# Moving small transfers to the end of a recurrence step, and splitting an attention product in two

## The chip, the cores and the metric

One core of one Trainium2 chip runs the whole kernel. The metric is the device time of one execution in microseconds (us). A ratio is the mean time of one kernel's fast runs divided by that of the kernel before in the same rounds on the same chip, so it is not quite the ratio of the medians quoted beside it. Intervals are 95%. Sets of experiments fell on different chips; therefore ratios, not times, are compared across sets.

## The reference

Half of the program is a recurrence over 64 segments of 32 tokens. Each segment's attention input has 8 memory rows ahead of its own 32, and the output's first 8 rows are the next segment's memory. The other half is an FFN, which the change does not touch.

```python
def _A_ref(x, mem0, Wq, Wk, Wv, Wo, seg_len):      # B=1, S=2048, Dm=1024, H=32, Dh=128, M=8, seg_len=32
    mem = mem0
    for s in range(n_seg):                         # 64 steps, each needs the mem of the one before
        h = jnp.concatenate([mem, x[:, s*32:(s+1)*32]], axis=1)
        q, k, v = (jnp.einsum('btd,dhe->bhte', h, W) for W in (Wq, Wk, Wv))
        scores = jnp.where(mask, jnp.einsum('bhqe,bhke->bhqk', q, k) * scale, -1e9)
        o = jnp.einsum('bhqk,bhke->bhqe', _softmax(scores), v)
        o = jnp.einsum('bhte,hed->btd', o, Wo)
        mem = o[:, :8].copy(); outs.append(o[:, 8:])
# ... b = gelu(x @ w_gate) * (x @ w_up) @ w_down;   out = g*a + (1-g)*b with g = sigmoid((x*gate_w).sum(-1))
```

## The kernel before

A step has two halves of 16 heads. Each weight matrix half is eight pieces of 512 KB. Not all 64 pieces fit in SBUF: 12 slots are shared by the two halves, and each of them is refilled once a step, when its first use in the step is over. These 12 pieces (6.3 MB) are the stream.

```python
PAIRS = {"k": (0, 2), "q": (0, 2), "v": (0, 1, 2, 4, 6), "o": (0, 2, 4)}      # pieces whose two halves share a slot
ORDER = (("k", 0), ("q", 0), ("v", 0), ("k", 1), ("q", 1), ("o", 0), ("v", 1), ("o", 1))
# half 0 takes the shared pieces first, half 1 takes them last; odd steps swap the halves
def spent(k):
    n = home[k]; done[n] += 1
    if done[n] < len(uses[n]) and uses[n][done[n]] != k:
        fetch(n)                                  # SP issues the next piece for this slot
```

Rows whose k, q and v do not depend on the recurrence (the last 8 of a segment, "rest" rows) are projected four segments at a time by extra PE work, the fills, spread over the steps. Their results go to DRAM scratch (qk_scr, v_scr) and come back when their segment is due (qkr, vB). So a step also has small transfers, all issued by POOL: hT, qkr (two), vB, a_scr, o_scr, the fill stores, and in some steps oR and hR.

The names: hT is the step's input, transposed; hR the rest rows of four segments; qkr and vB the rest rows' q and k, and v. tok is the copy of a projection's result that PE transposes into kT and qT; vA is that of v. E8 are the exponentials, pA and pB the softmax weights (pB for the rest columns), tA and tB their transposes. oT is attend's result, oRc its rest rows, which go to o_scr and come back as oR; a_scr takes the step's output rows, a_bf.

```python
def scores(r):                                    # ... PE: scores, DVE: max, subtract, ACT: exp into E8, DVE: sum, reciprocal
    pB <- E8 * sm (rest columns); pA <- E8 * sm; tA <- transpose(pA); tB <- transpose(pB)      # all DVE, in this order

def attend(u):
    def f(e):
        for j in range(4):
            for g in range(4):                    # main part: 16 matmuls with 32 rows
                e.matmul(PB[bo[g]][...], lhsT=vA[r, j, :], rhs=tA[...], start=(j == 0), stop=False)
        for g in range(4):                        # tail: the rest rows
            ins = e.matmul(PB[bo[g]][...], lhsT=vB[r, u, :], rhs=tB[...], start=False, stop=True)
        return ins
    op("pe", f, rd=[vA.r(), tA.r(), tB.r(), vB.r()], wr=[BK(b) for b in bo])
    # ... four copies to oT (ACT, DVE), one to oRc (POOL)

# a step's schedule: on(matrix, half, piece, work ahead of that piece)
on("k", 0, 5, lambda: load_v(s))
on("v", 0, 4, lambda: trans(qT))
on("k", 1, 3, lambda: rest_k(1))                  # POOL copies the rest keys from qkr into kT
on("q", 1, 0, lambda: load_h(s + 1))
on("q", 1, 1, lambda: load_qk(s + 1, 0))
on("v", 1, 2, lambda: load_qk(s + 1, 1))
on("q", 1, 4, lambda: trans(kT))
on("o", 0, 0, some(f1, 4)); on("o", 0, 0, lambda: attend(ua)); on("o", 0, 0, some(f1, 1))
on("o", 1, 0, lambda: rest_k(0))
on("o", 1, 0, some(f2, 5)); on("o", 1, 0, lambda: attend(ub)); on("o", 1, 0, some(f2))
```

"attend(0)" and "attend(1)" below are the first and the second attend of a step. A group of fill work is four matmuls.

## Time and profile before

| | before |
|---|---|
| median time | 2303.5 us (2301.8 to 2305.6, 4 runs) |
| time a step in the recurrence (steps 8 to 59) | 24.45 us |
| PE idle, 165 to 1660 us | 127.5 of 1495 us |
| bytes streamed a step | 6.3 MB in 12 pieces |

The window sums of the kernel before over most of the recurrence. Each column is an engine's busy time and, in brackets, its instructions; then the granted clock, the DMA share and the bandwidth.

```profile
core 0: us, PE busy (x) PEld busy (x) DVE busy (x) ACT busy (x) POOL busy (x), PEclk, DMA share, GB/s
165.00:1660.00 1495.00, 1367.52 (x31932) 778.54 (x31924) 568.19 (x1629) 430.30 (x982) 543.95 (x1011) 0.99 0.80 287
```

PE is busy 91% of the time, so a step is first of all a row of PE work, with about 2.1 us of gaps. What ends the gaps ahead of matmuls that read weight pieces is in the tile view of `sl` (us in total, times):

```profile
its engine sat idle before it (us, times) until:
  issue: 56.0, 61
  DMA sl<-in_A_Wq_dram: 18.4, 28
  DMA sl<-in_A_Wo_dram: 7.2, 13
  DMA sl<-in_A_Wv_dram: 6.8, 11
  ACT oT L576: 1.7, 4
  DMA sl<-in_A_Wk_dram: 1.3, 2
```

Pieces that come late cost 33.7 us. "Issue" is a gap in which no wait shows. Counted from the packed trace, 53 of the 61 lie between two matmuls of one piece, where the program has no wait at all, and all 61 end 1.2 to 1.6 us after the end of a 16 KB packet on the instruction queue (251 such packets in this window).

One step cut into five windows:

```profile
1142.00:1144.00 2.00, 1.52 (x26) 0.70 (x30) 0.34 (x2) 0.45 (x2) 0.74 (x2) 1.00 0.00 0
1144.00:1148.00 4.00, 4.00 (x76) 1.74 (x64) 0.42 (x1) 1.19 (x2) 2.93 (x6) 1.00 0.78 199
1148.00:1158.00 10.00, 10.00 (x282) 6.26 (x282) 5.17 (x14) 2.73 (x6) 2.39 (x5) 1.00 1.03 406
1158.00:1162.00 4.00, 3.99 (x99) 2.22 (x92) 2.88 (x9) 1.03 (x2) 2.75 (x5) 1.00 0.99 348
1162.00:1166.40 4.40, 3.84 (x113) 2.45 (x114) 0.90 (x4) 1.54 (x5) 2.29 (x5) 1.00 0.46 161
```

DMA is full (1.03, 0.99) in the middle of the step and idle (0.00) around its end. That idle stretch is what the change aims at. The DMA issues of the small loads show what they meet in the middle (KB each, median us from issue to landing):

```profile
qkr<-qk_scr POOLq DMA_DIRECT2D x128, 64.0 KB, 5.4
hT<-xq_scr POOLq DMA_DIRECT2D x64, 64.0 KB, 5.7
vB<-v_scr POOLq DMA_DIRECT2D x63, 64.0 KB, 6.0
```

And attend(1) on PE in the timeline (start us, us, then the instructions):

```profile
1160.76 1.25 PE L697 MATMUL pb<-sl,hR 128*32 128x512 bf16 x20
1161.94 0.27 PE L641 MATMUL pb<-tA,vA 32*128 32x40 bf16 x16
1162.06 0.19 PE L646 MATMUL pb<-tB,vB 32*128 32x64 bf16 x4
1162.18 0.83 PE L697 MATMUL pb<-sl,hR 128*32 128x512 bf16 x12
1162.84 2.18 PE L682 MATMUL pb<-sl,oT 128*32 128x256 bf16 x64
```

### The profile page before, as it was taken

What the parts mean: (1) busy time and instruction counts of PE and PEld (TensorE: products, weight loads), DVE (VectorE), ACT (ScalarE), POOL (GpSimd) and SP (SyncE); (2) the same over time, 40 slices, a digit from 0 to 9 for tenths busy, and PEclk for the clock granted to TensorE, in tenths of its full rate; (3) what the DMA queues carried; (4) which work ended last, traced back from release to release, by engine and by line L of the source; (5) the groups of instructions that cost most, each with busy time, mean ns of one, the idle gap of its engine ahead of it and who ended that gap; (6) DMA issues with size and microseconds to landing.
All of it is one profiled execution on the core that took longest, in us unless ns stands there. A gap on an engine that the chain in (4) does not pass through costs nothing.

```text
span 2304.5 us, 80168 instructions
## 1 busy us (share of the span) xinstructions
PE 2060.9 (89%) x36594; PEld 1099.2 (48%) x36614; DVE 901.2 (39%) x2164; ACT 604.1 (26%) x1280; POOL 616.0 (27%) x1107
## 2 busy tenths in 40 slices
PE   2588998899999998898998998998879999999998
PEld 1244555555555555555555455554444444444443
DVE  3134333334334343343343433333335164363452
ACT  1122232222323222232232322222223032131230
POOL 5233333343333433333333333333210000000000
PEclk9999999999999999999999999999999999999999
DMA  9968788788788787787887887887782802606206
GB/s 358 379 213 305 257 304 294 261 289 309 265 303 302 272 316 271 269 322 265 290 323 248 302 302 256 302 303 266 270 330 90 276 34 80 230 1 208 103 1 237
DMA packets 225714, 576.45 MB, mean 250 GB/s; under 512 B 30424, under 2 KB 42584, under 8 KB 225376
## 3 DMA queue, kind: packets, MB, share of 16 engines
q1 hardware_dynamic: 189536, 513.35, 61.7%
q0 software_dynamic: 26624, 44.14, 5.6%
q10 hardware_dynamic: 9216, 13.83, 1.7%
q8 instruction: 287, 4.70, 0.8%
q14 instruction: 51, 0.42, 0.1%
HBM read 539.71 MB, written 31.39 MB: 248 GB/s over the span
## 4 chain that ended last, share of the span: by engine, by line
PE 65%; DMA 24%; issue 5%; DVE 3%; ACT 2%; POOL 1%; SPq 0%; ACTq 0%; POOLq 0%; DVEq 0%
PE pb L670 20%; PE pb L929 14%; DMA sl<-in_A_Wq_dram 11%; PE pb L682 9%; PE pb L697 6%; PE pb L966 6%; DMA sl<-in_A_Wo_dram 5%; PE pb L712 3%; PE pb L588 3%; DMA sl<-in_A_Wv_dram 3%; DMA wd<-in_B_w_down_dram 2%; PE pb L609 1%; DMA xr_scr<-xr 1%; PE pb L641 1%; PE pb L603 1%
## 5 line engine op out<-in xcount | busy, mean ns | idle before, releaser
L670 PE MATMUL pb<-sl,hT 128*32 128x512 bf16 x12288 | 756.8, 383 | 43.2 <-DMA sl<-in_A_Wq_dram 18.4
L670 PEld LDWEIGHTS pb<-sl,hT 128*32 128x32 bf16 x12288 | 331.7, 97 | 327.2 <-DMA sl<-in_A_Wq_dram 38.8
L682 PE MATMUL pb<-sl,oT 128*32 128x256 bf16 x8192 | 281.8, 275 | 56.2 <-issue 46.1
L576 ACT ACTIVATE tok<-pb 128x512 bf16<-128x512 f32 x320 | 191.0, 597 | 458.0 <-PE pb L670 393.0
L682 PEld LDWEIGHTS pb<-sl,oT 128*32 128x32 bf16 x8192 | 213.0, 97 | 98.7 <-issue 54.6
L697 PE MATMUL pb<-sl,hR 128*32 128x512 bf16 x3072 | 215.0, 390 | 19.6 <-DMA sl<-in_A_Wq_dram 7.3
L929 PE MATMUL pb<-xT,wg 128*128 128x512 bf16 x896 | 213.2, 381 | 16.2 <-DVE GT L945 8.4
L655 POOL COPY oRc<-oT 128x128 bf16<-128x128 bf16 x128 | 98.6, 770 | 452.4 <-DVE oT L579 445.4
L929 PE MATMUL pb<-xT,wu 128*128 128x512 bf16 x896 | 211.7, 379 | 0.0
L966 PE MATMUL pb<-wd,GT 128*128 128x512 bf16 x876 | 194.7, 379 | 8.9 <-DMA wd<-in_B_w_down_dram 7.7
L579 DVE CAST oT<-pb 128x160 bf16<-128x160 f32 x256 | 71.2, 320 | 230.4 <-PE pb L646 230.4
L937 ACT ACTIVATE s<-pb 128x512 f32<-128x512 f32 x112 | 66.8, 596 | 326.8 <-PE pb L929 307.3
L929 PEld LDWEIGHTS pb<-xT,wg 128*128 128x128 bf16 x896 | 87.1, 98 | 125.1 <-DVE GT L945 12.8
L576 ACT ACTIVATE vA<-pb 128x512 bf16<-128x512 f32 x128 | 76.4, 597 | 265.9 <-PE pb L670 265.9
L966 PEld LDWEIGHTS pb<-wd,GT 128*128 128x128 bf16 x896 | 86.4, 98 | 117.2 <-DMA wd<-in_B_w_down_dram 15.5
L588 PE MATMUL pb<-ident,tok 128*128 128x128 bf16 x1280 | 128.1, 222 | 13.2 <-ACT tok L576 8.9
L929 PEld LDWEIGHTS pb<-xT,wu 128*128 128x128 bf16 x896 | 87.7, 98 | 105.9 <-issue 0.3
L938 DVE SCALAR_TENSOR_TENSOR tp<-s,pb 128x512 f32<-128x512 f32 x112 | 76.9, 687 | 155.2 <-ACT s L937 155.1
L588 PEld LDWEIGHTS pb<-ident,tok 128*128 128x128 bf16 x1280 | 72.6, 98 | 123.2 <-ACT tok L576 94.3
L579 DVE COPY kT<-pb 128x512 bf16<-128x512 bf16 x128 | 51.9, 405 | 197.9 <-PE pb L588 197.9
L614 DVE TENSOR_REDUCE st<-pb 128x8 f32<-128x320 f32 x128 | 62.9, 492 | 159.6 <-PE pb L609 159.6
L697 PEld LDWEIGHTS pb<-sl,hR 128*32 128x32 bf16 x3072 | 83.3, 98 | 81.5 <-DMA sl<-in_A_Wq_dram 8.4
(76 smaller groups left out, 1929.7 us busy)
## 6 DMA issues: line engine op xcount, KB each, us to landing
sl<-in_A_Wv_dram SPq DMA_DIRECT2D x331, 512.0 KB, 9.9
sl<-in_A_Wo_dram SPq DMA_DIRECT2D x205, 512.0 KB, 5.9
sl<-in_A_Wk_dram SPq DMA_DIRECT2D x142, 512.0 KB, 5.5
sl<-in_A_Wq_dram SPq DMA_DIRECT2D x142, 512.0 KB, 7.4
wd<-in_B_w_down_dram SPq DMA_DIRECT2D x56, 1024.0 KB, 6.4
qk_scr<-stg POOLq DMA_DIRECT2D x64, 128.0 KB, 5.8
qkr<-qk_scr POOLq DMA_DIRECT2D x128, 64.0 KB, 5.4
wg<-in_B_w_gate_dram SPq DMA_DIRECT2D x3, 1792.0 KB, 13.2
```

The source lines that it names most:

```text
L576: op("act", lambda e: e.activation(o, i, ACTF.Copy), rd=rd, wr=wr)
L579: op("dve", lambda e: e.tensor_copy(o, i), rd=rd, wr=wr)
L588: ins = e.transpose(PBV[TT][:, j * 128:(j + 1) * 128], tok[:, j * 128:(j + 1) * 128], ident[:, :])
L655: op("pool", lambda e: e.tensor_copy(oRc[:, u, :, :].rearrange("p c x -> p x c"), oT[:, :, :, 32:40].rearrange("p g j c -> p (g j) c")), r ...
L670: ins = e.matmul(PB[bk][32 * g:32 * g + 32, :], lhsT=h[:, i, :], rhs=w[:, g * 512:(g + 1) * 512], start=(p % 8 == 0), stop=(p % 8 == 7))
L682: ins = e.matmul(PB[XO][32 * g:32 * g + 32, 0:256], lhsT=oT[:, gp_, 2 * jj + hh, 0:32], rhs=w[:, c:c + 256], start=(r == 0 and p % 8 == 0 ...
L697: ins = e.matmul(PB[b][32 * g:32 * g + 32, :], lhsT=h[:, k[2], :], rhs=w[:, g * 512:(g + 1) * 512], start=(n == 0), stop=(n == 7))
L712: ins = e.matmul(PB[b][32 * g:32 * g + 32, 0:256], lhsT=t[:, :, 2 * i + hh], rhs=w[:, c:c + 256], start=(ends[0] and i == 0 and hh == 0), ...
L929: ins = e.matmul(PB[bk][:, 0:FB], lhsT=w[:, kc, cc:cc + 128], rhs=xT[:, :, :, kc, :].rearrange("p t i c -> p (t i) c"), start=(kc == 0), s ...
L937: op("act", lambda e, hg=hg: e.activation(s1[:, :], hg, ACTF.Square, scale=SQ), rd=[BK(bg)], wr=[s1.r()])
L938: op("dve", lambda e, hg=hg, t=t: e.scalar_tensor_tensor(out=t[:, :], in0=s1[:, :], scalar=1.0, in1=hg, op0=ALU.add, op1=ALU.mult), rd=[BK ...
L966: ins = e.matmul(PB[bank[2 * k + hf]][:, :], lhsT=GT[:, j, tb * 128:(tb + 1) * 128], rhs=w[:, jj, hf * 512:(hf + 1) * 512], start=(j == 0) ...
```

## The change

Its intent: issue the small loads, and the stores of v fills, from attend(1) on, where no piece streams; let attend's main part start before tB is ready, and put fill work between it and its tail; give two transposes one piece more of time; and repair the copy of the mem columns. In the kernel before, that copy's function looked its target up only when the program was emitted, after the loop, so that all 63 copies went into one of the two hT buffers. Its work and its waits were as planned, only its address was not.

```diff
@@ tiles: E8 gets a place that tA does not overlap
+        cur[0] += 128
         oT = al("oT", [128, 4, 4, LQ])
-        E8 = al("E8", [128, 8, LQ], at=qT.off + 384)
+        E8 = al("E8", [128, 8, LQ], at=qT.off + 512)
@@ scores(): DVE order
-            pB <- ...; pA <- ...; tA <- transpose(pA)
+            pA <- ...; tA <- transpose(pA); pB <- ...
             tB <- transpose(pB)
@@ attend(): two operations
+            op("pe", f, rd=[vA.r(), tA.r()], wr=[BK(b) for b in bo])
+        def attend_tail(u):
+            ...
-            op("pe", f, rd=[vA.r(), tA.r(), tB.r(), vB.r()], wr=[BK(b) for b in bo])
+            op("pe", f, rd=[tB.r(), vB.r()], wr=[BK(b) for b in bo])
@@ schedule of a step
-                on("k", 0, 5, lambda: load_v(s))
-            if s % 4 == 3 and G < NG:
-                on("k", 0, 5, lambda: load_r(G))
+            if s > 0:
+                on("k", 0, 6, lambda: rest_k(0))
-            on("v", 0, 4, lambda: trans(qT))
+            on("v", 0, 5, lambda: trans(qT))
-                on("q", 1, 0, lambda: load_h(s + 1))
-                on("q", 1, 1, lambda: load_qk(s + 1, 0))
-                on("v", 1, 2, lambda: load_qk(s + 1, 1))
-            on("q", 1, 4, lambda: trans(kT))
-            ... load_oR(Q, 1) at q(1), load_oR(Q, 0) at o(0)
+            on("q", 1, 5, lambda: trans(kT))
-            on("o", 0, 0, some(f1, 4))
+            on("o", 0, 0, some(f1, 2))
             on("o", 0, 0, lambda: attend(ua))
+            on("o", 0, 0, some(f1, 2))
+            on("o", 0, 0, lambda: attend_tail(ua))
-                on("o", 1, 0, lambda: rest_k(0))
-            on("o", 1, 0, some(f2, 5))
+            on("o", 1, 0, some(f2, 4))
             on("o", 1, 0, lambda: attend(ub))
+            on("o", 1, 0, some(f2, 2))
+            on("o", 1, 0, lambda: attend_tail(ub))
             on("o", 1, 0, some(f2))
+            ... load_qk(s + 1, 0), load_qk(s + 1, 1), load_v(s + 1), load_h(s + 2), load_r, load_oR, all at o(1)
+                if k2[0] == "v":
+                    on("o", 1, 3, lambda: fill_store(*k2, G, stage[1]))      # was in the next step
@@ mem columns
-                    op("dve", lambda e, t=t, bk=bk: e.tensor_copy(h_next[...], ...))
+                    op("dve", lambda e, t=t, bk=bk, h=h_next: e.tensor_copy(h[...], ...))
```

More of the change, by code (lines that the diff above doesn't have):

```diff
@@ L621, in scores @@
             op("dve", lambda e: e.reciprocal(sm, sm), rd=[st8.r(8, 16)], wr=[st8.r(8, 16)])
+            op("dve", lambda e: e.tensor_tensor(out=pA[:, :, :], in0=E8[:, :, 0:32], in1=b8(sm, 32), op=ALU.mult),
+               rd=[E8.r(), st8.r(8, 16)], wr=[pA.r()])
+            op("dve", lambda e: e.transpose(tA[:, :, :].rearrange("p a c -> p (a c)"), pA[:, :, :].rearrange("p a c -> p (a c)")),
+               rd=[pA.r()], wr=[tA.r()])
             op("dve", lambda e: e.tensor_tensor(
@@ L626, in scores @@
                rd=[E8.r(), st8.r(8, 16)], wr=[pB.r()])
-            op("dve", lambda e: e.tensor_tensor(out=pA[:, :, :], in0=E8[:, :, 0:32], in1=b8(sm, 32), op=ALU.mult),
-               rd=[E8.r(), st8.r(8, 16)], wr=[pA.r()])
-            op("dve", lambda e: e.transpose(tA[:, :, :].rearrange("p a c -> p (a c)"), pA[:, :, :].rearrange("p a c -> p (a c)")),
-               rd=[pA.r()], wr=[tA.r()])
             op("dve", lambda e: e.transpose(tB[:, :, :].rearrange("p a c -> p (a c)"), pB[:, 0:256]),
                rd=[pB.r()], wr=[tB.r()])
+        bo = (B0, B1, B2, SS)
         def attend(u):
-            bo = (B0, B1, B2, SS)
             def f(e):
@@ L640, in f @@
                         r = slice(32 * g, 32 * g + 32)
-                        e.matmul(PB[bo[g]][:, j * LQ:(j + 1) * LQ], lhsT=vA[r, j, :],
-                                 rhs=tA[r, 2 * j:2 * j + 2, :].rearrange("p a c -> p (a c)")[:, 0:LQ],
-                                 start=(j == 0), stop=False, skip_group_check=True)
+                        ins = e.matmul(PB[bo[g]][:, j * LQ:(j + 1) * LQ], lhsT=vA[r, j, :],
+                                       rhs=tA[r, 2 * j:2 * j + 2, :].rearrange("p a c -> p (a c)")[:, 0:LQ],
+                                       start=(j == 0), stop=False, skip_group_check=True)
+                return ins
+            op("pe", f, rd=[vA.r(), tA.r()], wr=[BK(b) for b in bo])
+        def attend_tail(u):
+            def f(e):
                 for g in range(4):
@@ L801, in bass_gated_mix__memory_aug_recurrent_mem_tr__geglu_ffn__prompt_kernel @@
                 on("k", 1, 0, lambda: (load_qk(0, 1), load_v(0, slice(1, 2)), load_r(1) if NG > 1 else None))
-            else:
-                on("k", 0, 5, lambda: load_v(s))
-            if s % 4 == 3 and G < NG:
-                on("k", 0, 5, lambda: load_r(G))
+                on("q", 1, 0, lambda: load_h(1))
+            if s > 0:
+                on("k", 0, 6, lambda: rest_k(0))
             on("q", 0, 0, lambda: evac(bank_of["k", 0], tok))
@@ L813, in bass_gated_mix__memory_aug_recurrent_mem_tr__geglu_ffn__prompt_kernel @@
             on("q", 1, 0, lambda: evac(bank_of["k", 1], tok))
-            if not last:
-                on("q", 1, 0, lambda: load_h(s + 1))
-                on("q", 1, 1, lambda: load_qk(s + 1, 0))
-                on("v", 1, 2, lambda: load_qk(s + 1, 1))
-            on("q", 1, 4, lambda: trans(kT))
-            if s % 4 == 0 and Q >= 0:
-                on("q", 1, 2, lambda: load_oR(Q, 1))
-            if s % 4 == 1 and Q >= 0:
-                on("o", 0, 3, lambda: load_oR(Q, 0))
+            on("q", 1, 5, lambda: trans(kT))
             def add_part():
@@ L845, in bass_gated_mix__memory_aug_recurrent_mem_tr__geglu_ffn__prompt_kernel @@
             on("o", 1, 0, lambda: evac(bank_of["v", 1], vA))
-            if not last:
-                on("o", 1, 0, lambda: rest_k(0))
-            on("o", 1, 0, some(f2, 5))
-            on("o", 1, 0, lambda: attend(ub))
-            on("o", 1, 0, some(f2))
+            on("o", 1, 0, some(f2, 4))
+            on("o", 1, 0, lambda: attend(ub))
+            on("o", 1, 0, some(f2, 2))
+            on("o", 1, 0, lambda: attend_tail(ub))
+            on("o", 1, 0, some(f2))
+            if not last:
+                on("o", 1, 0, lambda: load_qk(s + 1, 0))
+                on("o", 1, 0, lambda: load_qk(s + 1, 1))
+                on("o", 1, 0, lambda: load_v(s + 1))
+                if s + 2 < NSEG:
+                    on("o", 1, 0, lambda: load_h(s + 2))
+            if s % 4 == 2 and G + 1 < NG:
+                on("o", 1, 0, lambda: load_r(G + 1))
+            if s % 4 == 0 and Q >= 0:
+                on("o", 1, 0, lambda: load_oR(Q, 1))
+            if s % 4 == 1 and Q >= 0:
+                on("o", 1, 0, lambda: load_oR(Q, 0))
             if k2:
                 on("o", 1, 1, lambda: fill_evac(*k2, F2, stage[1]))
+                if k2[0] == "v":
+                    on("o", 1, 3, lambda: fill_store(*k2, G, stage[1]))
             def o_store(s=s):
@@ L872, in bass_gated_mix__memory_aug_recurrent_mem_tr__geglu_ffn__prompt_kernel @@
                        rd=[a_bf.r(128 * t, 128 * t + 128), ident.r()], wr=[BK(bk)])
-                    op("dve", lambda e, t=t, bk=bk: e.tensor_copy(
-                        h_next[:, :, NR:32].rearrange("p (g t) c -> p t g c", t=2)[:, t],
+                    op("dve", lambda e, t=t, bk=bk, h=h_next: e.tensor_copy(
+                        h[:, :, NR:32].rearrange("p (g t) c -> p t g c", t=2)[:, t],
                         PBV[bk][:, 0:128].rearrange("p (g c) -> p g c", g=4)[:, :, NR:32]),
@@ L882, in store @@
                    wr=[("D", "a", s)], lane="st")
-                if k2:
+                if k2 and k2[0] == "q":
                     fill_store(*k2, G, stage[1])
```

## The prediction

> **What bounds the kernel now.** The recurrence is 64 steps; the transposes that end a step (L871) run from 140.3 to 1659.4 us in the source view: 24.5 us a step, about 1,565 us of 2,304.8. The rest, mostly FFN, is untouched. Window sums over 165 to 1660 us: PE busy 1367.5 of 1495.0 us (91%), DMA share 0.80. So a step is PE-bound with about 2.1 us of PE idle. The view of the weight pieces' tile names it: 33.7 us of waits for pieces (Wq 18.4, Wo 7.2, Wv 6.8, Wk 1.3) and 56.0 us of "issue" in 61 pauses. These lie mostly inside a piece, often in attend(0)'s Wo matmuls, and end about 1.4 us after a 16 KB instruction packet lands: PE seems to wait for instructions. The Trainium skill ("Runtime: NRT & Kernel Launch", "Instruction fetch mechanics") calls block crossings "mostly hidden"; here they do not look so.
>
> DMA carries 12 pieces (6.3 MB) a step. In the window sums of one step it is saturated (0.83 to 1.05, up to 418 GB/s) for about 18 us, then nearly idle for about 4. The POOL queue takes 5.6% of the engines, about 2.0 us a step, of which I count about 1.5 in the saturated stretch. The skill ("DMA: Bandwidth & Descriptors", "Issuing engines are not separate DMA queues") says that all queues share the 16 engines; the trace agrees: piece bandwidth dips to about 330 GB/s when small loads pass.
>
> **What changes.**
> - Gain 1: loads of hT, qkr, vB, oR, hR and v stores leave the stream. POOL issues each in 0.55 us (timeline), so they start after attend(1)'s oRc copy, about 2 us before the next k pieces; about half fits in the idle time. I expect 0.5 to 0.7 us less small traffic in the stream, and 60% of the 34 us of piece waits removed, more from v and o than from q (the spill lands early in the next stream): 20 us.
> - Gain 2: transposes one piece (0.22 us) later: most of 8.9 us of waits for tok: 8 us.
> - Gain 3: attend needs no tB, and tA comes about 0.25 us earlier: 7 us.
> - Gain 4: slightly shorter instruction stalls: 8 us.
> - Loss 1: the split. Groups of four fill matmuls start 216 ns apart, 322 ns into attend, and about 0.1 us is lost leaving it. Four more shape switches a step of about 0.1 us: 25 us, partly hidden where a piece is waited for.
> - Loss 2: two fill groups (0.43 us), not three, between tail and attend(1)'s Wo: oT's evacuation (626 ns from tail to Wo without fills) shows by 0.07 us a step, vA by 0.05: 7 us.
> - Loss 3: rest_k(0) queues on POOL behind loads, o_scr, v stores (2.2 us for four) and a_scr, and kT's copy on DVE follows it: up to 0.3 us in half of the steps, 5 us.
> - The mem-column correction moves no work.
>
> Gains 43, losses 37 with 8 hidden: net about 13 us faster.
>
> **Prediction: 2292 us, 2262 to 2322.** Faster by over 2%: 0.11. Within 2%: 0.86. Slower by over 2%: 0.03.
>
> **What would show it.** Right: POOL-queue traffic moves from mid-step to the idle end; waits for Wv and Wo more than halve, Wq less; PE waits for tok fall; attend shows two more switches of about 0.1 us each; waits for oT before attend(1)'s Wo rise; issue pauses stay near 50 us.
>
> **What would make it wrong.** Issue pauses halving or growing (their places move with the instruction count); switches that cost nothing because PE waits anyway; late POOL work (rest_k, a_scr before pA) becoming a PE wait; Wq waits vanishing wholly.

## The result and the profile after

| | before | after |
|---|---|---|
| median time | 2303.5 us | 2312.5 us (2310.1 to 2315.6, 4 runs) |
| ratio | 1 | 1.004 (1.0022 to 1.0057) |
| time a step (steps 8 to 59) | 24.45 us | 24.70 us |
| PE idle, 165 to 1660 us | 127.5 us | 108.4 us |

The change makes the kernel 0.4% slower, although PE idles less. The same views as above, now of the changed kernel. First the window sums:

```profile
core 0: us, PE busy (x) PEld busy (x) DVE busy (x) ACT busy (x) POOL busy (x), PEclk, DMA share, GB/s
165.00:1660.00 1495.00, 1386.59 (x31807) 772.10 (x31810) 575.96 (x1619) 428.49 (x976) 523.14 (x1002) 1.00 0.81 286
```

PE is busy 19 us more in the same 1495 us, yet it gets through fewer matmuls (31807 against 31932). Its work itself has become longer. The waits ahead of weight pieces:

```profile
its engine sat idle before it (us, times) until:
  issue: 49.8, 53
  DMA sl<-in_A_Wq_dram: 20.7, 31
  DMA sl<-in_A_Wo_dram: 2.9, 6
  DMA sl<-in_A_Wv_dram: 2.0, 3
  ACT oT L577: 1.4, 3
  DMA sl<-in_A_Wk_dram: 0.8, 2
```

Waits for Wv and Wo fell from 14.0 to 4.9 us; those for Wq did not fall. The same step in windows at the same places:

```profile
1155.50:1157.50 2.00, 1.52 (x31) 0.68 (x26) 0.34 (x2) 0.45 (x2) 1.77 (x4) 1.00 0.39 102
1157.50:1161.50 4.00, 4.00 (x80) 1.84 (x68) 0.00 (x0) 1.19 (x2) 4.00 (x8) 1.00 0.87 216
1161.50:1171.50 10.00, 9.31 (x222) 5.31 (x214) 5.24 (x14) 2.73 (x6) 1.68 (x5) 1.00 1.02 400
1171.50:1175.50 4.00, 4.00 (x129) 3.08 (x133) 3.00 (x9) 0.57 (x2) 1.58 (x3) 1.00 0.85 318
1175.50:1179.90 4.40, 4.01 (x117) 2.36 (x105) 0.98 (x3) 1.99 (x6) 2.91 (x6) 1.00 0.56 187
```

The step's end now carries data (0.39 where there was 0.00), and POOL is busy from end to end of the second window. The small loads find the engines free and land in less than half the time:

```profile
qkr<-qk_scr POOLq DMA_DIRECT2D x128, 64.0 KB, 2.2
hT<-xq_scr POOLq DMA_DIRECT2D x64, 64.0 KB, 2.5
vB<-v_scr POOLq DMA_DIRECT2D x63, 64.0 KB, 2.4
```

The moved loads do what they were meant to do. Attend(1) on PE:

```profile
1175.12 1.06 PE L704 MATMUL pb<-sl,hR 128*32 128x512 bf16 x16
1176.12 0.27 PE L643 MATMUL pb<-tA,vA 32*128 32x40 bf16 x16
1176.32 0.61 PE L704 MATMUL pb<-sl,hR 128*32 128x512 bf16 x8
1176.87 0.21 PE L653 MATMUL pb<-tB,vB 32*128 32x64 bf16 x4
1177.01 0.61 PE L704 MATMUL pb<-sl,hR 128*32 128x512 bf16 x8
1177.49 1.93 PE L689 MATMUL pb<-sl,oT 128*32 128x256 bf16 x64
```

The same work from the first fill to the first Wo matmul takes 2.37 us (1175.12 to 1177.49) where it took 2.08. To measure such losses apart from waits I used the start times in the trace. For each kind of neighbouring PE groups I took the lower quartile of the interval from start to start over steps 8 to 59, and added these up for a step: an estimate of PE's undisturbed step. The rest of the step is waiting of any kind, but a wait that comes back in most steps counts as undisturbed. (Another grouping of the matmuls gives 21.96 and 22.37 us where the table has 22.09 and 22.50: the level depends on it, the rise of 0.41 does not.)

| us a step | step | undisturbed | rest |
|---|---|---|---|
| before | 24.45 | 22.09 | 2.36 |
| after | 24.70 | 22.50 | 2.21 |

The undisturbed sum rose by 0.41 us, and the waits fell by only 0.15. Fill groups start 216 ns apart; a fill and the attend behind it 322 ns, and so do a fill and the tail; attend's main part and the fill behind it 203 ns, where main part and tail are 114 ns apart; tail and fill 137 ns, before 124. One attend thus takes 322 + 203 + 322 + 137 - (322 + 114 + 124 + 216) = 208 ns more, about 0.1 us at each of its two new borders, of which a step has four.

### The profile page after: what moved, and what is told of

Same layout as the page of the kernel before. It is cut to its first block, busy times and chain, and to the rows that moved or that the text cites. A ratio compares the mean times of both kernels' runs of the same rounds, so it can differ in the third digit from the quotient of the medians.

```text
span 2313.8 us, 80025 instructions
## 1 busy us (share of the span) xinstructions
PE 2089.5 (90%) x36614; PEld 1097.2 (47%) x36614; DVE 913.6 (39%) x2164; ACT 604.5 (26%) x1280; POOL 599.5 (26%) x1107
## 4 chain that ended last, share of the span: by engine, by line
PE 69%; DMA 20%; issue 4%; DVE 3%; POOL 2%; ACT 2%; SPq 0%; ACTq 0%; POOLq 0%; DVEq 0%
PE pb L677 20%; PE pb L943 14%; DMA sl<-in_A_Wq_dram 12%; PE pb L689 10%; PE pb L704 8%; PE pb L980 7%; PE pb L719 3%; PE pb L589 3%; DMA sl<-in_A_Wo_dram 2%; DMA wd<-in_B_w_down_dram 2%; DMA sl<-in_A_Wv_dram 1%; PE pb L610 1%; PE pb L643 1%; DMA xr_scr<-xr 1%; PE pb L604 1%
## 5 line engine op out<-in xcount | busy, mean ns | idle before, releaser
L704 PE MATMUL pb<-sl,hR 128*32 128x512 bf16 x3072 | 233.2, 395 | 17.0 <-DMA sl<-in_A_Wq_dram 6.8
L956 DVE SCALAR_TENSOR_TENSOR tp<-tp,pb 128x512 f32<-128x512 f32 x112 | 77.0, 688 | 78.8 <-ACT tp L955 78.8
```

The source lines that it names most:

```text
L704: ins = e.matmul(PB[b][32 * g:32 * g + 32, :], lhsT=h[:, k[2], :], rhs=w[:, g * 512:(g + 1) * 512], start=(n == 0), stop=(n == 7))
L956: op("dve", lambda e, hu=hu, t=t: e.scalar_tensor_tensor(out=t[:, :], in0=t[:, :], scalar=1.0, in1=hu, op0=ALU.add, op1=ALU.mult), rd=[BK( ...
```

## The experiments

Two theories stood at first. Theory 1: the split is the loss, its switches of the PE array's shape. Theory 2: the switches are hidden behind the waits for pieces, and the loss is POOL's late work and the small loads that spill into the next stream.

### First set: the parts alone

**a_merged**: the changed kernel with attend and tail together again.

```diff
-            on("o", 0, 0, some(f1, 2)); attend(ua); some(f1, 2); attend_tail(ua)
+            on("o", 0, 0, some(f1, 4)); attend(ua); attend_tail(ua)
-            on("o", 1, 0, some(f2, 4)); attend(ub); some(f2, 2); attend_tail(ub)
+            on("o", 1, 0, some(f2, 5)); attend(ub); attend_tail(ub)
```

> The changed kernel with the tail put straight after the main part of attend again (four fill pieces before it in attend(0), five in attend(1), as before); all else of the change stays. Theory 1 (the split is the loss): the trace of after shows the sum of the undisturbed intervals between PE groups up by 0.41 us a step, four switches of 0.1 us; take it away and about 26 us go, less a few us of waits that reappear: 2286 to 2296 us, below the kernel before. Theory 2 (the split is hidden behind waits for pieces, and the late POOL work and the small loads that spill into the next stream are the loss): 2308 to 2314 us.

Measured: 2296.7 us, ratio 0.9971 (0.9934 to 1.0008). The loss is gone, as Theory 1 has it, but the median lies just above what it expected: something else in this kernel still cost time.

**b_split**: the kernel before with the split (two operations, new softmax order, padding and E8's place, fills spread), nothing else.

> The kernel before with the split alone (main part and tail apart, fill pieces spread as in the change, tA made before pB, E8 moved by 128 bytes); no load is moved, the transposes stay. Theory 1: 0.41 us a step longer, minus what the earlier tA and the waits for pieces hide: 2318 to 2330 us. Theory 2: 2300 to 2307 us.

Measured: 2332.6 us, ratio 1.012 (1.0084 to 1.0155), the undisturbed sum 22.49 us. Theory 2 falls. The loss of 28 us is a little over the 26 us that 0.41 us in 64 steps makes, although I had expected some of it to be hidden.

**loads_only**: the kernel before with the moved transfers, the moved rest_k and the repaired mem columns.

> The kernel before with the moved loads and stores, the moved rest_k and the corrected mem columns alone; attend whole, softmax order and transposes as before. Theory 1: the gain of the moved loads without the cost of the split: 2288 to 2298 us. Theory 2: 2307 to 2314 us, slower than before.

Measured: 2290.4 us, ratio 0.9926 (0.9886 to 0.9966), the undisturbed sum 22.08 us. The moved loads gain, alone, about what I had given them.

**mem_only**: the repaired mem columns alone.

> The kernel before with the corrected mem columns alone (each step's copy goes to that step's own hT instead of all to one). Both theories: the same work and the same waits, 2300 to 2307 us. The reference comparison should come out closer than that of the kernel before.

Measured: 2308.2 us, ratio 1.001 (0.9971 to 1.0049): no time in it. The comparison with the reference said only "correct" for both, so that the second half of the expectation is not answered. The record calls nostream below "correct" too, whose result is wrong: that word proves little here.

### Second set: what the stream costs, and the smaller terms

**nostream**: the kernel before, but no slot is ever fetched a second time. Its output is wrong, which doesn't matter for the time.

```diff
-            if done[n] < len(uses[n]) and uses[n][done[n]] != k:
-                fetch(n)
```

> The kernel before without any second fetch of a weight piece (the result is wrong on purpose): DMA is idle but for the small loads. Waits for pieces are then zero. Theory A (the issue pauses inside pieces are PE waiting for instructions that compete with the stream): pauses fall from 56 us to under 15, a step takes 22.1 to 22.8 us, total 2160 to 2205 us. Theory B (instruction supply is too slow by itself, or the pauses have another cause): about 50 us of pauses stay, a step takes 23.3 us or more, total 2220 us or more. The sum of undisturbed PE intervals stays at 22.1 us.

Measured: 2149.4 us, ratio 0.9324; a step takes 22.27 us, of which 22.09 are undisturbed. Of all the idle time ahead of weight pieces there is left:

```profile
its engine sat idle before it (us, times) until:
  ACT oT L574: 2.1, 5
```

The 56 us of issue pauses are gone with the stream, to the last one. Theory A is right, by more than it expected. The pauses are thus caused by the stream; together with their place behind the instruction packets this makes PE waiting for instructions the likely reading. The stream does not make the packets themselves longer: all 287 take 1.05 us on average in the kernel before and 1.10 us here. If PE waits for instructions, it is because packets come late, which no view shows. A second thing matters for the prediction: the small waits for other engines stay as they were. In the waits of PE (us in total, times, longest), first before, then nostream:

```profile
PE pb L641 <- issue: 3.7, 5, 1.1
PE pb L641 <- ACT vA L576: 2.8, 4, 0.7
PE pb L588 <- ACT tok L576: 1.4, 3, 0.5
```

```profile
PE pb L639 <- ACT vA L574: 3.4, 5, 0.7
PE pb L586 <- ACT tok L574: 1.9, 4, 0.5
```

They are not made by the stream, they are just small: 1.4 us for tok and 2.8 us for vA in the whole window, and before attend's main part (L641) PE waits neither for tA nor for tB.

**trans_late**: loads_only with the two transposes one piece later.

> The moved loads alone, with the two transposes one piece later as in the change. My prediction gave that 8 us. Theory A (the waits for tok were real and go): ratio about 0.989. Theory B (tok was ready anyway; the wait passes to the next limit): ratio 0.991 to 0.996, and PE's idle time before the transposes stays within 3 us of loads_only's.

Measured: 2288.5 us, ratio 0.9924 (0.9898 to 0.9951), against 0.9926 of loads_only: Theory B. The two ran on different chips and their intervals would let 8 us (0.35%) pass; the trace is firmer. PE's idle time before the transposes was 7.1 us in loads_only (tok 1.9) and 3.6 us here (tok 1.9 again).

**rest_early**: loads_only with rest_k(0) ahead of the a_scr store, and the v stores back in the next step.

```diff
-                on("k", 0, 6, lambda: rest_k(0))
+                on("k", 0, 3, lambda: rest_k(0))
-                if k2[0] == "v":
-                    on("o", 1, 3, lambda: fill_store(*k2, G, stage[1]))
-                if k2 and k2[0] == "q":
+                if k2:
                     fill_store(*k2, G, stage[1])
```

> The moved loads alone (attend whole), with rest_k(0) one place before the a_scr store on POOL and the v stores back behind it in the next step, as in the kernel before. In loads_only the first transposes of v(0) waited 0.25 us on average in every fourth step (s mod 4 = 2), where rest_k stood behind four v stores. Theory A (the late rest_k holds up kT's copy and so PE): that wait goes, and the time falls 3 to 8 us below loads_only's ratio of 0.9926, to about 0.990. Theory B (the wait is by chance): ratio 0.992 to 0.995.

Measured: 2287.4 us, ratio 0.9927 (0.9900 to 0.9955): no gain, which is Theory B's number, though Theory A's wait is real. In the waits of DVE (us in total, times, longest), loads_only has kT's copy behind POOL's rest_k:

```profile
DVE kT L579 <- PE pb L588: 107.6, 36, 4.6
DVE kT L579 <- POOL kT L756: 83.6, 20, 4.6
```

and rest_early has it behind PE's transposes alone:

```profile
DVE kT L579 <- PE pb L588: 191.7, 63, 4.9
```

The wait went and the time did not. Steps with s mod 4 = 2 took 24.56 us in loads_only and 25.11 us in rest_early; but two more traces of loads_only (pair_loads and base4, below) have 24.83 and 24.77. That the wait was handed on to the next limit is not shown.

**one_split**: the changed kernel with only attend(1) split.

> The changed kernel with attend(0) whole and only attend(1) split: half of the extra switches. If the cost is the switches, the sum of undisturbed PE intervals is 22.29 us a step (22.09 whole, 22.50 with both split) and the time lies between that of the changed kernel (ratio 1.004) and that with both whole (0.997): 0.998 to 1.003. If one of the two splits alone were the loss (the fewer fill pieces behind attend(1)'s tail), the ratio is at one of the two ends.

Measured: 2309.9 us, ratio 1.0031 (1.0000 to 1.0061), the undisturbed sum 22.32 us, halfway as expected. The time is just above the expected range. The interval leaves open whether the second split costs more than half.

### Third set: the pieces side by side on one chip

> The kernel loads_only once more, as the base of this set on one chip: ratio 0.990 to 0.996 if the gain of the moved loads is real on another chip too.

Measured, **pair_loads** (loads_only again): 2281.1 us, ratio 0.9888 (0.9855 to 0.9922).

> The changed kernel itself on this chip. Split (1.012) times moved loads (0.9926) gives 1.0045 if the two simply add and the rest of the change is worth nothing; 1.000 or less would mean that the two interact or that the later transposes or the softmax order gain.

Measured, **pair_after** (the changed kernel again): 2314.7 us, ratio 1.0048 (1.0023 to 1.0074). Split times moved loads, 1.0045, meets it: within the interval the two add, and the rest of the change is worth nothing.

**sm_first**: pair_loads with tA made first, E8 moved, the padding, and the tail as its own operation straight behind the main part.

> pair_loads with tA made before pB and E8 moved by 128 bytes, and the tail as its own operation straight behind the main part: the split's preparation without its switches. If the earlier tA gains (prediction: 7 us), about 0.3% below pair_loads; if the wait before attend is bound by the vA copy, the same within 0.2%; if the reordering is what kept a_merged at 0.9971, about 0.4% above pair_loads.

Measured: 2297.4 us, ratio 0.9982 (0.9955 to 1.0009). It was 16 us slower by the medians (0.95% by the ratios) than pair_loads on the same chip, without a single new switch (undisturbed 22.09 us). My prediction had given this part 7 us of gain. So there was a second loss within the split, and the third set did not say which edit made it.

**best**: rest_early and trans_late together.

> The combination that the runs so far point to: moved loads, attend whole, old softmax order, later transposes, rest_k(0) ahead of the a_scr store, v stores behind it. Expected 0.2 to 0.4% below pair_loads if the late rest_k costs what the trace of loads_only shows (0.25 us in every fourth step), else equal to it; in both cases faster than the kernel before and than the changed kernel.

Measured: 2282.5 us, ratio 0.9896 (0.9870 to 0.9922). It beats both kernels and equals pair_loads.

### Fourth set: which edit of the preparation costs

> loads_only once more as the base of this set: ratio 0.988 to 0.994.

Measured, **base4** (loads_only again): 2286.2 us, ratio 0.9917 (0.9893 to 0.9941).

**pad_only**: base4 and one line.

```diff
+        cur[0] += 128
         oT = al("oT", [128, 4, 4, LQ])
```

> loads_only with 128 bytes of padding before oT and nothing else: oT, tok, stage, pA, pB and 11 of the 12 streamed slots lie 128 bytes higher. Theory P (the address shift slows the streaming): ratio about 0.7 to 0.9% above base4, and longer waits for Wq pieces. Theory S (softmax order): within 0.3% of base4.

Measured: 2294.7 us, ratio 0.9963 (0.9939 to 0.9988), which is 0.46% (0.9963/0.9917), about 11 us, above base4. The waits for Wq did not grow as Theory P had said (10.8 us against 10.3). Over all traces this sign is unclear: 10.8 to 21.7 us in the five padded kernels with moved loads and attend in place, 9.0 to 15.2 in the seven unpadded ones.

**sep_tail**: base4 with the tail as an operation of its own, in place.

> loads_only with the tail as an operation of its own, straight behind the main part of attend; softmax order, addresses and fill pieces as in base4. Expected within 0.2% of base4 under both theories; 0.7% above it if the separate operation is the loss.

Measured: 2286.6 us, ratio 0.9925 (0.9898 to 0.9951): nothing.

**switches**: base4 with main part and tail apart, two fill groups between, no padding, old softmax order.

> loads_only with attend and tail apart as in the change (two fill pieces between), but no padding and the old softmax order. If the four switches cost what the trace shows and none of it is hidden: 26 us, 1.1% above base4. If 9 us of it are hidden (pair_after against sm_first: 17 us): 0.7% above. The undisturbed PE sum is 22.49 us.

Measured: 2299.9 us, ratio 0.9990 (0.9962 to 1.0018), 0.74% or 17 us above base4. The undisturbed sum is 22.50 us, against 22.09 of base4. The page's line on PE's busy time over the whole span shows it too. First base4, then switches:

```profile
PE 2061.1 (90%) x36594; PEld 1103.6 (48%) x36614; DVE 903.1 (40%) x2164; ACT 604.1 (26%) x1280; POOL 598.0 (26%) x1107
```

```profile
PE 2081.8 (91%) x36594; PEld 1093.5 (48%) x36614; DVE 903.2 (39%) x2164; ACT 604.0 (26%) x1280; POOL 597.6 (26%) x1107
```

The same number of matmul records takes 20.7 us more. About 9 of the 26 us are hidden: the rest of the step falls from 2.13 to 2.00 us. It is not the waits for pieces that shrink (16.6 us in base4, 19.2 here) but the issue pauses: 57.5 us in base4, 47.0 here.

### Fifth set: padding or softmax order

> pad_only once more: 0.994 to 0.998 of the kernel before if the padding's loss is real; 0.989 to 0.993 (as the unpadded kernels) if pad_only's loss was chance.

Measured, **pad_two** (pad_only again): 2301.9 us, ratio 0.9972 (0.9943 to 1.0001).

> sm_first once more: padding plus the new softmax order. If the order costs nothing, equal to pad_two within 0.2%; if it costs half of what sm_first lost, 0.4 to 0.5% above pad_two; if the earlier tA gains the predicted 7 us, 0.3% below.

Measured, **sm_two** (sm_first again): 2298.1 us, ratio 0.9973 (0.9943 to 1.0004), equal to pad_two. Within the intervals (0.3% each) the softmax order costs nothing and gains nothing; the padding is the second loss. All measurements with moved loads and attend in place agree on it:

| address of the slots | ratios to the kernel before |
|---|---|
| unpadded (7 measurements, 5 kernels) | 0.9888, 0.9896, 0.9917, 0.9924, 0.9925, 0.9926, 0.9927 |
| 128 bytes higher (5 measurements, 3 kernels) | 0.9963, 0.9971, 0.9972, 0.9973, 0.9982 |

The means are 0.58%, or 13 us, apart. How the padding costs is not settled. By the kernel's allocation, 11 of the 12 streamed slots start at a multiple of 256 bytes in the kernel before and 128 bytes beyond one with the padding; tok, pA and others move too, and no run moved the slots alone. The Trainium skill ("DMA: Bandwidth & Descriptors", "How a descriptor splits into AXI transactions") says that a transaction must start at a 256-byte boundary, so that a descriptor which starts beyond one begins at the boundary below it, and the bytes ahead of its start are fetched too. By this rule a row of 4,096 bytes would take 17 transactions in place of 16 (an estimate from that page). The page words it for reads, though, and the padding moves what the loads write. The direction agrees, and about 0.5% is what these runs show. The traces do show slower packets: of the 4,096-byte packets on the queue of the weight pieces, 86 to 87% took 159 ns or less in the seven unpadded traces and 71 to 73% in the five padded ones (80% in the kernel before, 52% in b_split). So the padding slows the stream; the mean packet hardly moves (175.7 to 176.8 ns, 176.5 to 177.7 with padding), so that this does not explain the size of the loss, and that the slots are the cause is my guess. The FFN's tiles move too, but its part of the trace is nearly as long in both (613 to 617 us, 615 to 620 with padding): most of the loss lies in the recurrence.

## Why the prediction was right or wrong

I predicted 2292 us and "about 13 us faster"; it is 9 us slower. The range and the class "within 2%" hold, the direction does not. That the number is only about 20 us off is partly luck: gains of 23 us that did not come stand against losses of 12 us that did not come either, and a loss of about 11 us was not in the sum.

- **Bound and place of the time: right.** The step is PE work with about 2 us of disturbance, and nostream shows that nearly all of this disturbance comes from the stream.
- **Gain 1, moved loads, 20 us: right.** Three measurements of loads_only give ratios 0.9926, 0.9888 and 0.9917, or 17 to 26 us. The POOL queue's traffic moved to the step's end, and waits for Wv and Wo more than halved. That Wq falls less was right for the moved loads alone (18.4 to 9.0, 10.3 and 13.0 us) and too hopeful for the changed kernel, where it rose to 20.7. All waits for pieces fell from 33.7 to 13.3, 16.6 and 19.8 us in the loads_only traces, but only to 26.4 in the changed kernel.
- **Loss 1, switches, 25 us with 8 hidden: right in size.** Four switches of 0.1 us each are in the trace (0.41 us a step), and 17 us net are measured by switches against base4. The hiding place was wrong: I named waits for pieces, and the issue pauses shrank. The Trainium skill ("TensorEngine Tiling (Array Packing)", "Key Properties") says that a change of tiling mode drains the array; the trace agrees as far as it shows a loss of about 0.1 us at these borders (128*32 to 32*128 and back), not what makes it.
- **The step that failed: "Gains 43".** Gains 2, 3 and 4, together 23 us, were not found. Gain 2 (later transposes, 8 us): trans_late is level with loads_only. The wait was mis-sized. The 8.9 us stand in this line of the page, which covers the whole execution:

```profile
L588 PE MATMUL pb<-ident,tok 128*128 128x128 bf16 x1280 | 128.1, 222 | 13.2 <-ACT tok L576 8.9
```

Of them 7.1 us lie before 165 us, mostly in the extra fills of step 0, which the change does not touch, and only 1.4 us in the window of the other steps (165 to 1660 us). Gain 3 (earlier tA, 7 us): sm_two is level with pad_two, and before attend PE waited 2.8 us for vA and not at all for tA or tB. Gain 4 (shorter instruction stalls, 8 us): the pauses did not shrink in the kernels with moved loads alone (61.9, 60.9 and 57.5 us, before 56.0). In the kernels with moved loads and a split attend they did (49.8 and 48.3 us in the changed kernel), but this fall comes with the split and is most likely what hides part of Loss 1, which the sum had already counted as "8 hidden". So I had taken two gains from waits that were never there in the steps, and, it seems, one gain twice.
- **Loss 2 and Loss 3, 12 us: not found.** rest_k's delay is in the trace, but rest_early removed it and gained nothing. Waits for oT before Wo did not rise (1.7 us before, 1.4 after), and the fewer fills behind the tail are within the 17 us of switches.
- **A term that was missing: the padding, about 11 us** (13 over all measurements). I read `cur[0] += 128` as bookkeeping for E8 and did not ask what else it moves.

The measured terms close: 0.9917 (moved loads) times 1.0074 (switches) times 1.0046 (padding) is 1.0036, and the changed kernel measured 1.0040 and 1.0048. Likewise switches times padding is 1.0120, the ratio of b_split. Each factor has an interval of some 0.3%, so that so close a fit is partly luck. In microseconds: about 20 gained by the moved loads, 17 lost by the switches and 11 by the padding make 8 us slower, where 9 were measured. What stays open is the mechanism of the padding, and whether the split of attend(1) costs more than that of attend(0).

## What to carry to other kernels

Moving small transfers out of the stretch where DMA is full pays about what the piece waits show; judge it apart from the edits that come with it. On an engine that is 91% busy, count each border where its mode changes as work, because it stays when the waits go; and before a wait is counted as a gain, read it in the window of the steps that the edit changes, not from the line of the whole page. When an edit shifts an allocation, measure the shift alone.

## What the Trainium skill lacked or had wrong

- "Runtime: NRT & Kernel Launch", "Instruction fetch mechanics": crossing a 16 KB instruction block is called mostly hidden. With DMA saturated, PE pauses put down to "issue" came to 56.0 us in 61 pauses, and to none without the stream, where the page's word fits (258 packets in the window); that they are instruction waits is inferred from this and from the packets 1.2 to 1.6 us ahead of each.
- "TensorEngine Tiling (Array Packing)", "Key Properties": the drain at a mode change is named without a cost. Here the border costs about 0.1 us (322 ns against 216 ns from group to group).
- "DMA: Bandwidth & Descriptors", "How a descriptor splits into AXI transactions": the 256-byte rule is given in transactions and beats, without a time for large loads, and for reads only. Moving the slots and some tiles by 128 bytes cost about 0.5% of this kernel; the runs do not show that this rule is the reason.
- "DMA: Bandwidth & Descriptors", "Latency and other measured facts": says that the fixed cost of a DMA is smaller under a lighter HBM load, but has no time for a small load beside a running stream: 64 KB landed in 5.4 to 6.0 us within the stream and in 2.2 to 2.5 us outside it.
